# A 1x1 depthwise-separable layer on one core: chunk steps, weight loads in halves, a dummy matmul loop, ScalarE emptying PSUM, and a few stores in uneven pieces

## The chip, the cores and the metric

The kernel runs on one NeuronCore of a Trainium2 chip. The metric is the device time of one execution in microseconds (us). A run gives one such time; the number for the kernel is the median of several runs. Separately, one execution is recorded by the hardware profiler, and its span runs from the first to the last instruction of that execution.

## The reference

The input x has shape (1, 384, 384, 384) in bf16, dw is (1, 1, 384) and pw is (384, 384). Cut to what matters for a 1x1 depthwise kernel, the reference is:

```python
def reference(x, dw, pw):              # k = 1, pad = 0
    out = x * dw[0, 0][None, None, None, :]
    return jnp.einsum('bhwc,cd->bhwd', out, pw)
```

Each of the 147,456 pixels is a row of 384 channels; every channel is scaled by its dw, and the row is multiplied by the 384 x 384 matrix pw. The kernel folds dw into the rows of pw once, so that one matrix product of x with the scaled weights is left. x and the output are 113 MB each.

## The kernel before, in words

The pixels are cut into 288 supertiles of 512. Supertiles are grouped into chunks, which are the unit of DMA. `_chunks` gives the chunk sizes in supertiles: 1, 1, 2, 4, then 34 chunks of `LMAX` = 8, then 4, 2, 1, 1, which are 42 chunks. A chunk of x lies in one of three buffers `Xs`, a chunk of the output in one of three buffers `Os`. A full chunk is 3 MB in each direction.

SyncE (SP) issues the loads and stores of chunks. After the first three loads its order is written out: `load_x(t + 3)`, then `store(t)`, for t from 0. `load_x` (L95) waits on `s_t`, the semaphore of the last transpose of chunk t, since that frees the x buffer. `store` waits on `s_d` (L105) and `s_a` (L107), which say that VectorE and ScalarE have emptied PSUM for the chunk's last supertile. The completion of a store counts on `s_o`, and the engines wait for it before they write that output buffer again, three chunks later (L210, L211).

In a supertile the channels must come to the partitions. VectorE does this with 32 x 32 stream transposes of pairs of bf16 values read as uint32 (L174): two instructions for each supertile, h = 0 and h = 1, each for half of the six channel blocks, into one of two buffers `Ts`. TensorE then runs 48 matmuls per supertile (L134): six blocks, two parities of channel, four row groups q, each matmul with 32 rows and 384 columns. The four row groups work in the array beside each other and write four banks of PSUM. Even supertiles use one half of PSUM (`PS[0]`), odd ones the other. After the matmuls VectorE copies bank 3 to the output buffer (L212) and ScalarE copies banks 0 to 2 (L215), both casting to bf16.

TensorE's instructions are a hardware loop over pairs of supertiles. Ahead of a supertile's blocks 0 and 3 it waits for the transposes (`s_t`, L133); its first matmul waits on `s_a`, and the first matmul of row group 3 on `s_d`, so that PSUM is free. Every half of a supertile adds one to `s_pe`, for which the copies and the transposes wait.

Ahead of the loop the weights are made. Four DMAs of 288 KB (L89, two on SP, two on ScalarE's queue) bring pw to four groups of 32 partitions, a small one (L112) brings dw. VectorE spreads dw into `dwsel` (L186), transposes supertile 0, waits for all four weight DMAs, and makes six of the twelve scaled pieces `w_r` (L197); ScalarE makes the other six (L199). VectorE then transposes supertile 1. TensorE waits for all twelve pieces.

Of the kernel before, what the change touches and what calls it, by code (L numbers as in the profile page):

```python
# [7 lines left out]
BF16 = mybir.dt.bfloat16  # L8
F32 = mybir.dt.float32
U32 = mybir.dt.uint32  # L10
COPY = mybir.ActivationFunctionType.Copy

LMAX = 8
NX = 3
NO = 3


def _chunks(n_super: int):

    head, tail = [1, 1, 2, 4], [4, 2, 1, 1]  # L20
    mid = n_super - sum(head) - sum(tail)
    assert mid > 0 and mid % LMAX == 0
    return head + [LMAX] * (mid // LMAX) + tail
# [3 lines left out]
def kernel(  # L27
# [11 lines left out]
    nc = tc.nc  # L39
    P = nc.NUM_PARTITIONS  # L40
    B, H, W, C = x.shape
    assert dw.shape[0] == 1 and dw.shape[1] == 1, "only k=1 depthwise supported"
    D = pw.shape[1]
    N = B * H * W
    assert C == 384 and D == 384 and N % 1024 == 0
    NB = C // 64

    xf = x.rearrange("b h w c -> (b h w) c")
    of = out.rearrange("b h w d -> (b h w) d")

    NS = N // 512
    chunks = _chunks(NS)
    NT = len(chunks)
    s0 = [sum(chunks[:t]) for t in range(NT)]

    consts = ctx.enter_context(tc.tile_pool(name="consts", bufs=1))
# [3 lines left out]
    pw_r = consts.tile([P, NB, 2, D], BF16, name="pw_r")  # L60
    w_r = consts.tile([P, NB, 2, D], BF16, name="w_r")
    dwt = consts.tile([32, NB, 2], BF16, name="dwt")
    dwsel = consts.tile([P, NB * 2], F32, name="dwsel")
    warm = consts.tile([P, 3], F32, name="warm")
    seed = consts.tile([P, 2], F32, name="seed")

    Xs = [bufp.tile([P, 4 * LMAX, C], BF16, name=f"X{i}") for i in range(NX)]
    Ts = [bufp.tile([P, NB, 256], BF16, name=f"T{i}") for i in range(2)]
    Os = [bufp.tile([P, 4 * LMAX * D], BF16, name=f"O{i}") for i in range(NO)]
# [3 lines left out]
    s_t = [[nc.alloc_semaphore(f"s_t{i}{h}") for h in range(2)] for i in range(2)]  # L73
    s_pe = nc.alloc_semaphore("s_pe")
    s_a = [nc.alloc_semaphore(f"s_a{i}") for i in range(2)]
    s_d = [nc.alloc_semaphore(f"s_d{i}") for i in range(2)]
    s_o = [nc.alloc_semaphore(f"s_o{i}") for i in range(NO)]
    s_dw = nc.alloc_semaphore("s_dw")
    s_pw = nc.alloc_semaphore("s_pw")
    s_ds = nc.alloc_semaphore("s_ds")  # L80
    s_wr = nc.alloc_semaphore("s_wr")
    s_seed = nc.alloc_semaphore("s_seed")

    with tc.tile_critical():  # L84
        pw_v = pw.rearrange("(b w r) d -> w b (r d)", w=32, r=2)
        dw_v = dw.rearrange("a e (b w r) -> w (a e b) r", w=32, r=2)

        def load_pw(eng, q):
            eng.dma_start(pw_r[32 * q : 32 * q + 32].rearrange("w b r d -> w b (r d)"), pw_v).then_inc(s_pw, 16)  # L89

        def load_x(t):
            L = chunks[t]
            r = 512 * s0[t]
            src = xf[r : r + 512 * L, :].rearrange("(p s) c -> p (s c)", p=P)
            d = nc.sync.dma_start(Xs[t % NX][:, : 4 * L, :].rearrange("p s c -> p (s c)"), src)  # L95
            if t >= NX:
                je = s0[t - NX] + chunks[t - NX] - 1
                d._wait_ge(s_t[je % 2][1], je // 2 + 1)
            d.then_inc(s_x[t % NX], 16)

        def store(t):
            L = chunks[t]
            r = 512 * s0[t]
            je = s0[t] + L - 1
            nc.sync.wait_ge(s_d[je % 2], je // 2 + 2)  # L105
            dst = of[r : r + 512 * L, :].rearrange("(q p j) d -> p q (j d)", q=4, p=P)
            d = nc.sync.dma_start(dst, Os[t % NO][:, : 4 * L * D].rearrange("p (q e) -> p q e", q=4))  # L107
            d._wait_ge(s_a[je % 2], je // 2 + 2)
            d.then_inc(s_o[t % NO], 16)


        nc.scalar.dma_start(dwt[:], dw_v).then_inc(s_dw, 16)  # L112
        load_x(0)
        load_pw(nc.scalar, 2)
        load_pw(nc.sync, 0)
        load_pw(nc.scalar, 3)
        load_pw(nc.sync, 1)
        for t in range(1, NX):
            load_x(t)
        for t in range(NT):  # L120
            if t + NX < NT:
                load_x(t + NX)
            store(t)
        for o in range(NO):
            nc.sync.wait_ge(s_o[o], 16 * len(range(o, NT, NO)))


        def supertile(s, rv):
            for b in range(NB):
                for par in range(2):  # L130
                    for q in range(4):
                        if par == 0 and q == 0 and b in (0, 3):
                            nc.tensor.wait_ge(s_t[s][b // 3], rv)  # L133
                        mm = nc.tensor.matmul(  # L134
                            PS[s][:, q, :D],
                            lhsT=Ts[s][32 * q : 32 * q + 32, b, par::2],
                            rhs=w_r[32 * q : 32 * q + 32, b, par, :],
                            start=(b == 0 and par == 0),
                            stop=(b == NB - 1 and par == 1),
                            tile_position=(32 * q, 0),  # L140
                        )
                        if b == 0 and par == 0 and q == 0:
                            mm._wait_ge(s_a[s], rv)
                        elif b == 0 and par == 0 and q == 3:
                            mm._wait_ge(s_d[s], rv)
                        if b in (2, 5) and par == 1 and q == 3:
                            mm.then_inc(s_pe)

        nc.tensor.wait_ge(s_wr, 2 * NB)
        with nc.tensor.Fori(0, NS // 2, 1) as it:  # L150
            rv = nc.tensor.to_reg(it + 1)
            for s in range(2):
                supertile(s, rv)


        for s in range(2):
            nc.vector.memset(seed[:, s : s + 1], 0.0).then_inc(s_d[s])  # L157
        nc.gpsimd.memset(warm[:], 0.0).then_inc(s_seed)  # L158
        for s in range(2):
            c = nc.scalar.copy(warm[:, s + 1 : s + 2], warm[:, 0:1])  # L160
            if s == 0:
                c._wait_ge(s_seed, 1)
            c.then_inc(s_a[s])

        def transposes(t, j):
            jj = s0[t] + j
            L = chunks[t]
            s = jj % 2
            Xw = Xs[t % NX][:].bitcast(U32)[:, : 4 * L, :].rearrange("p (k l) c -> p k l c", l=L)
            Tw = Ts[s][:].bitcast(U32).rearrange("p b (i k) -> p b k i", k=4)  # L170
            for h in range(2):
                if h == 0 and j == 0:
                    nc.vector.wait_ge(s_x[t % NX], 16 * (t // NX + 1))  # L173
                ins = nc.vector.transpose(  # L174
                    out=Tw[:, 3 * h : 3 * h + 3],
                    in_=Xw[:, :, j, 96 * h : 96 * h + 96].rearrange("p k (b w) -> p b k w", w=32),
                )
                if jj >= 2:
                    ins._wait_ge(s_pe, 2 * (jj - 2) + h + 1)
                ins.then_inc(s_t[s][h])  # L180

        order = [(t, j) for t in range(NT) for j in range(chunks[t])]

        nc.vector.wait_ge(s_dw, 16)
        for q in range(4):
            nc.vector.tensor_copy(  # L186
                dwsel[32 * q : 32 * q + 32, :], dwt[:].rearrange("w b r -> w (b r)")
            ).then_inc(s_ds)
        transposes(*order[0])
        for b in range(NB):  # L190
            for r in range(2):
                eng = nc.vector if r == 0 else nc.scalar
                if b == 0:
                    eng.wait_ge(s_pw, 64)  # L194
                sc = dwsel[:, 2 * b + r : 2 * b + r + 1]
                if r == 0:
                    i = nc.vector.tensor_scalar_mul(w_r[:, b, r, :], pw_r[:, b, r, :], sc)  # L197
                else:
                    i = nc.scalar.activation(w_r[:, b, r, :], pw_r[:, b, r, :], COPY, scale=sc)  # L199
                if b == 0:  # L200
                    i._wait_ge(s_ds, 4)
                i.then_inc(s_wr)
        transposes(*order[1])

        for jj, (t, j) in enumerate(order):
            L = chunks[t]
            s = jj % 2
            Ov = Os[t % NO][:, : 4 * L * D].rearrange("p (q j d) -> p q j d", q=4, d=D)
            if j == 0 and t >= NO:
                nc.vector.wait_ge(s_o[t % NO], 16 * (t // NO))  # L210
                nc.scalar.wait_ge(s_o[t % NO], 16 * (t // NO))  # L211
            e = nc.vector.tensor_copy(Ov[:, 3, j, :], PS[s][:, 3, :D])  # L212
            e._wait_ge(s_pe, 2 * jj + 2)
            e.then_inc(s_d[s])
            a = nc.scalar.copy(Ov[:, 0:3, j, :], PS[s][:, 0:3, :D])  # L215
            a._wait_ge(s_pe, 2 * jj + 2)
            a.then_inc(s_a[s])
            if jj + 2 < NS:
                transposes(*order[jj + 2])


# [28 lines left out]
```

## Time and profile before

| | |
|---|---|
| median of 3 runs | 586.94 us (586.64 to 588.1) |
| profiled execution, own time | 585.78 us |
| profiled execution, span | 584.0 us |
| mean granted TensorE clock | 0.996 |
| moved by DMA | 227.79 MB, mean 390 GB/s |
| transposes on VectorE (L174) | 576, 449.1 us busy |
| casts on VectorE (L212) | 288, mean 558 ns |
| casts on ScalarE (L215) | 288, mean 1119 ns |
| store of a full chunk, issue to landing | median 23.0 us |
| load of a full chunk, issue to landing | median 17.9 us |

The page gives an engine's busy time as the union of its instructions' spans. In lines of the timeline the first number is the start in us from the span's start, the second the length; in brackets is how long the engine had been idle and who ended that. The chain of waits is followed back from the last instruction. "L134" is a line of the kernel as printed above. A DMA's time to landing runs from its issue until the last of its data is reported.

### The profile page before, as it was taken

To read this page: it belongs to the slowest core of one execution; us is meant where nothing else is said; L and a number is where in the kernel's file an instruction comes from. 1 tells how busy PE (TensorE), PEld (TensorE's weight loads), DVE (VectorE), ACT (ScalarE), POOL (GpSimd) and SP (SyncE) were. 2 spreads that over 40 slices of the span, in tenths; PEclk is the share of its full clock that TensorE was granted. 3 is DMA by queue.
4 is the path that set the end of the run, shared out by engine and by line. 5 is a ranking of instruction groups with operands and counts; after the bars stand their busy time and mean duration, and the time that the engine had idled before them with its cause. 6 is when DMAs were issued, how large, how long until landed. Compare 5 with 4: busy or idle time off the path is not lost.

```text
span 584.0 us, 29852 instructions
## 1 busy us (share of the span) xinstructions
PE 563.9 (97%) x13824; PEld 412.6 (71%) x13824; DVE 563.9 (97%) x876; ACT 326.9 (56%) x297; POOL 0.3 (0%) x5
## 2 busy tenths in 40 slices
PE   1999999999999999999999999999999999999995
PEld 0667777777777777777777777777777777777773
DVE  3899999999999999999999999999999999999995
ACT  3555555555555656565655555555555555555553
POOL 0000000000000000000000000000000000000000
PEclk9999999999999999999999999999999999999998
DMA  8799999999999999999999999999999999999858
GB/s 289 253 424 425 428 422 421 410 396 404 402 396 411 378 412 411 394 402 413 391 407 395 414 414 396 404 419 396 404 397 403 389 424 397 389 403 407 333 221 311
DMA packets 29277, 227.79 MB, mean 390 GB/s; under 512 B 1616, under 2 KB 5456, under 8 KB 24656
## 3 DMA queue, kind: packets, MB, share of 16 engines
q1 hardware_dynamic: 28640, 227.09, 97.1%
q10 hardware_dynamic: 624, 0.59, 0.4%
q14 instruction: 12, 0.10, 0.0%
q8 instruction: 1, 0.02, 0.0%
HBM read 114.43 MB, written 113.25 MB: 390 GB/s over the span
## 4 chain that ended last, share of the span: by engine, by line
PE 93%; DMA 5%; ACT 1%; SPq 0%; issue 0%; DVE 0%; ACTq 0%; DVEq 0%
PE ps L134 93%; DMA X<-in_x_dram 2%; DMA out_dram<-O 1%; DMA pw_r<-in_pw_dram 1%; ACT O L215 1%; ACT w_r L199 1%; DVE T L174 0%; SPq L89 0%; SPq L107 0%; SPq L95 0%; SPq L245 0%; DVEq L173 0%; ACTq L211 0%; ACTq L194 0%; SPq L84 0%
## 5 line engine op out<-in xcount | busy, mean ns | idle before, releaser
L134 PE MATMUL ps<-w_r,T 32*128 32x384 bf16 x13824 | 563.9, 322 | 13.8 <-ACT w_r L199 12.8
L134 PEld LDWEIGHTS ps<-w_r,T 32*128 32x128 bf16 x13824 | 412.6, 93 | 164.8 <-issue 14.4
L215 ACT CAST O<-ps 128x1152 bf16<-128x1152 f32 x288 | 322.2, 1119 | 245.2 <-PE ps L134 243.3
L174 DVE STREAM_TRANSPOSE T<-X 128x384 uint32<-128x384 uint32 x576 | 449.1, 856 | 1.6 <-DMA X<-in_x_dram 1.6
L212 DVE CAST O<-ps 128x384 bf16<-128x384 f32 x288 | 160.7, 558 | 6.8 <-PE ps L134 4.6
L199 ACT ACTIVATE w_r<-pw_r,dwsel 128x384 bf16<-128x384 bf16 x6 | 3.1, 601 | 5.4 <-DMA pw_r<-in_pw_dram 5.4
L186 DVE CAST dwsel<-dwt 32x12 f32<-32x12 bf16 x4 | 0.7, 163 | 3.9 <-DMA dwt<-in_dw_dram 3.8
L197 DVE TENSOR_SCALAR w_r<-pw_r,dwsel 128x384 bf16<-128x384 bf16 x6 | 1.5, 312 | 2.1 <-DMA pw_r<-in_pw_dram 2.1
L160 ACT ACT_TABLE_LOAD x1 | 1.3, 1283 | 2.3 <-issue 2.3
L157 DVE MEMSET seed<- 128x1 f32 x2 | 0.1, 59 | 1.0 <-SPq L84 1.0
L160 ACT COPY warm<-warm 128x1 f32<-128x1 f32 x2 | 0.3, 190 | 0.0
L234 POOL MEMSET const-bfloat16-1.0<- 128x1 bf16 x1 | 0.1, 102 | 0.0
L234 POOL MEMSET const-uint8-127<- 128x1 uint8 x1 | 0.1, 101 | 0.0
L158 POOL MEMSET warm<- 128x3 f32 x1 | 0.1, 100 | 0.5 <-SPq L84 0.5
L234 POOL MEMSET const-float32-0.0<- 128x1 f32 x1 | 0.1, 98 | 0.2 <-issue 0.2
L234 POOL MEMSET const-float32-1.0<- 128x1 f32 x1 | 0.1, 98 | 0.0
## 6 DMA issues: line engine op xcount, KB each, us to landing
X<-in_x_dram SPq DMA_DIRECT2D x34, 3072.0 KB, 17.9
out_dram<-O SPq DMA_DIRECT2D x34, 3072.0 KB, 23.0
X<-in_x_dram SPq DMA_DIRECT2D x2, 1536.0 KB, 12.4
out_dram<-O SPq DMA_DIRECT2D x2, 1536.0 KB, 13.5
X<-in_x_dram SPq DMA_DIRECT2D x4, 384.0 KB, 5.7
X<-in_x_dram SPq DMA_DIRECT2D x2, 768.0 KB, 10.1
out_dram<-O SPq DMA_DIRECT2D x4, 384.0 KB, 3.8
out_dram<-O SPq DMA_DIRECT2D x2, 768.0 KB, 11.3
```

Source lines behind the costliest of these rows:

```text
L134: mm = nc.tensor.matmul(PS[s][:, q, :D], lhsT=Ts[s][32 * q : 32 * q + 32, b, par::2], rhs=w_r[32 * q : 32 * q + 32, b, par, :], start=(b = ...
L157: nc.vector.memset(seed[:, s : s + 1], 0.0).then_inc(s_d[s])
L158: nc.gpsimd.memset(warm[:], 0.0).then_inc(s_seed)
L160: c = nc.scalar.copy(warm[:, s + 1 : s + 2], warm[:, 0:1])
L174: ins = nc.vector.transpose(out=Tw[:, 3 * h : 3 * h + 3], in_=Xw[:, :, j, 96 * h : 96 * h + 96].rearrange("p k (b w) -> p b k w", w=32),)
L186: nc.vector.tensor_copy(dwsel[32 * q : 32 * q + 32, :], dwt[:].rearrange("w b r -> w (b r)")).then_inc(s_ds)
L197: i = nc.vector.tensor_scalar_mul(w_r[:, b, r, :], pw_r[:, b, r, :], sc)
L199: i = nc.scalar.activation(w_r[:, b, r, :], pw_r[:, b, r, :], COPY, scale=sc)
L212: e = nc.vector.tensor_copy(Ov[:, 3, j, :], PS[s][:, 3, :D])
L215: a = nc.scalar.copy(Ov[:, 0:3, j, :], PS[s][:, 0:3, :D])
L234: nc = _bacc.Bacc("TRN2", target_bir_lowering=False, num_devices=1)
```

## The change

Six things are changed together.

- The chunk sizes become 1, 1, 2, 2, 3, 3, 4, then 32 chunks of 8, then 6, 4, 3, 2, 1, which are 44 chunks.
- pw is loaded in eight DMAs rather than four: each of the four partition groups gets blocks 0 to 2 and blocks 3 to 5 apart, with a semaphore for each half. VectorE makes nine of the twelve scaled pieces, ScalarE three; dwsel is spread by ScalarE. TensorE waits for a piece where it first uses it: in even supertiles the first row group's matmul of every block and parity carries such a wait.
- Ahead of its loop TensorE runs 11 times 8 matmuls on a tile of zeros, which GpSimd has set.
- ScalarE empties all four banks of a supertile. VectorE empties two banks of the very last supertile alone.
- The last chunk's store is cut in two, one part issued by SP, one by ScalarE.
- Of the chunks with eight supertiles those with t % 4 == 1 (eight chunks) are stored by four DMAs, of 112, 7, 7 and 2 partitions.

```diff
-    head, tail = [1, 1, 2, 4], [4, 2, 1, 1]
+    head, tail = [1, 1, 2, 2, 3, 3, 4], [6, 4, 3, 2, 1]
...
-        def load_pw(eng, q):
-            eng.dma_start(pw_r[32 * q : 32 * q + 32].rearrange("w b r d -> w b (r d)"), pw_v).then_inc(s_pw, 16)
+        def load_pw(eng, q, h):
+            bs = slice(3 * h, 3 * h + 3)
+            eng.dma_start(
+                pw_r[32 * q : 32 * q + 32, bs].rearrange("w b r d -> w b (r d)"), pw_v[:, bs]
+            ).then_inc(s_pw[h], 16)
...
+        parts = {t: [(0, P)] for t in range(NT)}
+        for t in range(NT):
+            if chunks[t] == LMAX and t % 4 == 1:
+                parts[t] = [(0, 112), (112, 119), (119, 126), (126, 128)]
...
-            nc.sync.wait_ge(s_d[je % 2], je // 2 + 2)
...
+            nc.sync.wait_ge(s_a[je % 2], je // 2 + 2)
+            for lo, hi in parts[t]:
+                nc.sync.dma_start(dst[lo:hi], src[lo:hi]).then_inc(s_o[t % NO], 16)
...
-        load_pw(nc.scalar, 2)
-        load_pw(nc.sync, 0)
-        load_pw(nc.scalar, 3)
-        load_pw(nc.sync, 1)
+        for h in range(2):
+            for q in range(2):
+                load_pw(nc.scalar, 2 + q, h)
+                load_pw(nc.sync, q, h)
...
+        nc.sync.dma_start(of_last[:, 2:4], o_last[:, 2:4])._wait_ge(s_d, 1).then_inc(
+            s_last, 16
+        )
...
+        wr_eng = {(b, r): int(r == 1 and b % 2 == 0) for b in range(NB) for r in range(2)}
...
                         if b == 0 and par == 0 and q == 0:
                             mm._wait_ge(s_a[s], rv)
-                        elif b == 0 and par == 0 and q == 3:
-                            mm._wait_ge(s_d[s], rv)
+                        elif s == 0 and q == 0:
+                            mm._wait_ge(*wr_done[b, par])
...
-        nc.tensor.wait_ge(s_wr, 2 * NB)
+        nc.tensor.wait_ge(s_zero, 1)
+        with nc.tensor.Fori(0, 11, 1) as _:
+            for i in range(8):
+                nc.tensor.matmul(
+                    PS[1][:, i % 4, :D],
+                    lhsT=zero[32 * (i % 4) : 32 * (i % 4) + 32, 0:P],
+                    rhs=zero[32 * (i % 4) : 32 * (i % 4) + 32, :],
+                    start=True,
+                    stop=True,
+                    tile_position=(32 * (i % 4), 0),
+                )
+        nc.tensor.wait_ge(*wr_done[0, 0])
...
+        nc.gpsimd.memset(zero[:].bitcast(U32), 0).then_inc(s_zero)
...
+        nc.scalar.wait_ge(s_dw, 16)
         for q in range(4):
-            nc.vector.tensor_copy(
-                dwsel[32 * q : 32 * q + 32, :], dwt[:].rearrange("w b r -> w (b r)")
-            ).then_inc(s_ds)
+            nc.scalar.copy(dwsel[32 * q : 32 * q + 32, :], dwt[:].rearrange("w b r -> w (b r)")).then_inc(s_ds)
...
-                nc.vector.wait_ge(s_o[t % NO], 16 * (t // NO))
-                nc.scalar.wait_ge(s_o[t % NO], 16 * (t // NO))
-            e = nc.vector.tensor_copy(Ov[:, 3, j, :], PS[s][:, 3, :D])
-            e._wait_ge(s_pe, 2 * jj + 2)
-            e.then_inc(s_d[s])
-            a = nc.scalar.copy(Ov[:, 0:3, j, :], PS[s][:, 0:3, :D])
+                nc.scalar.wait_ge(s_o[t % NO], o_count[t % NO][t // NO])
+            nq = 4
+            if jj + 1 == NS:
+                nq = 2
+                nc.vector.wait_ge(s_o[t % NO], o_count[t % NO][t // NO])
+                e = nc.vector.tensor_copy(Ov[:, nq:4, j, :], PS[s][:, nq:4, :D])
+                e._wait_ge(s_pe, 2 * jj + 2)
+                e.then_inc(s_d)
+            a = nc.scalar.copy(Ov[:, 0:nq, j, :], PS[s][:, 0:nq, :D])
...
+        nc.scalar.dma_start(of_last[:, 0:2], o_last[:, 0:2])._wait_ge(s_a[(NS - 1) % 2], (NS - 1) // 2 + 2).then_inc(
+            s_last, 16
+        )
```

## The prediction

> **What bounds the kernel now.** I read the page's busy times first.
>
> ```profile
> PE 563.9 (97%) x13824; PEld 412.6 (71%) x13824; DVE 563.9 (97%) x876; ACT 326.9 (56%) x297; POOL 0.3 (0%) x5
> ```
>
> TensorE and VectorE tie, and the DMA row is full as well, so this line alone doesn't say who leads. The timeline of a steady stretch does:
>
> ```profile
> 300.77 1.12 ACT L215 CAST O<-ps 128x1152 bf16<-128x1152 f32 x1 [0.83 <-PE ps L134]
> 300.77 0.56 DVE L212 CAST O<-ps 128x384 bf16<-128x384 f32 x1
> 301.24 1.56 DVE L174 STREAM_TRANSPOSE T<-X 128x384 uint32<-128x384 uint32 x2
> 302.72 1.12 ACT L215 CAST O<-ps 128x1152 bf16<-128x1152 f32 x1 [0.83 <-PE ps L134]
> 302.72 0.56 DVE L212 CAST O<-ps 128x384 bf16<-128x384 f32 x1
> ```
>
> VectorE's cast starts with ScalarE's, and ScalarE waited 0.83 us for TensorE: both are released by the same matmul, so TensorE paces. The pitch is 1.95 us a supertile. VectorE can go faster: just after the stall at 31 us its casts come at 31.83 and 33.67, a pitch of 1.84, so it has about 0.1 us to spare. Next the chain of waits in order of time, which shows where TensorE doesn't run:
>
> ```profile
> 1.88 7.37 DMA pw_r<-in_pw_dram
> ...
> 9.34 3.15 ACT w_r L199 x6
> 12.49 0.32 issue
> 12.81 4.02 PE ps L134 x42
> ...
> 18.45 11.88 DMA X<-in_x_dram
> ...
> 30.43 0.87 DVE T L174
> 31.30 0.14 issue
> 31.44 538.40 PE ps L134 x13248
> ...
> 571.01 7.67 DMA out_dram<-O
> ...
> 578.76 1.12 ACT O L215
> ```
>
> The reader is to see a head (weights land at 9.25, ScalarE scales six pieces until 12.49, the first supertile takes 4.02 instead of 1.95), one stall for x at 31.4, then 538 us of unbroken TensorE, and a tail where the last cast waits for an output buffer. 288 x 1.95 = 561.6 us can't be touched here; some 22 us around it can.
>
> Last, the stores' time from issue to landing, from the view of tile O for 40 to 100 us and for 400 to 520 us:
>
> ```profile
> DMA to landing us min/median/max: 18.9/19.5/19.7
> DMA to landing us min/median/max: 24.7/25.1/25.4
> ```
>
> Latency grows steadily although demand is constant. The trace's semaphore arrivals say why: of a store's 16 arrivals the last comes 0.5 us after the middle one for the store issued at 32 us, 1.3 at 48 us, 9.5 at 501 us. One DMA engine falls behind. Its arrivals for the 30 stores between 67.3 and 541.8 us are 15.82 us apart, while a full chunk is computed in 15.6. It hurts nothing yet: a load has two chunks (31.2 us) before it is needed, an output buffer as long.
>
> **What the Trainium skill says.** "TensorE: Matmul & The Clock Gate", Part 1, gives N/2.4 + 2.5 ns for a warm matmul and N/1.2 for a cold one: 162.5 ns for N = 384. Four row groups run together, so 12 x 162.5 = 1.95 us, exactly the trace's pitch; the cold first supertile (4.02) agrees with 12 x 320 = 3.84. "ScalarE: Activation LUTs", What ACT_TABLE_LOAD costs, gives 0.833 ns an element and 186 ns fixed: 1.146 us for 1152, trace 1.119. "DMA: Bandwidth & Descriptors", Why a DMA increments its semaphore by 16 and not by 1, says that a DMA from SP uses the largest k up to 16 engines that divides its outer dimension, the lowest-numbered ones; no DMA of 7 partitions is in this trace. The same page, Latency and other measured facts, says engines 7 and 15 are usually slower than the rest; it blames another kind of queue, and the trace gives no engine numbers, but one straggler of 16 fits.
>
> **The change, part by part.**
>
> *ScalarE empties PSUM.* VectorE loses 287 casts of 0.558 us. That work lay beside TensorE: worth nothing in the steady state. ScalarE's cast grows from 1152 to 1536 elements: 1.119 + 384 x 0.833 ns = 1.44 us (upper bound, in proportion, 1.49). TensorE wants the bank group back 1.95 us after ScalarE was released, so 0.45 us stays; cost 0. ScalarE is then at 74%. The wait for the cast of VectorE goes from TensorE and from SP. Transposes may now run earlier; TensorE was never late for them outside the one stall.
>
> *Waits on TensorE.* Eleven more on weights in every even supertile, 1584 in all, satisfied after the first pass. The four waits of a supertile today leave no mark, since 12 x 162.5 is all of the 1.95; less than 1 ns each, so 0 to 1.6 us. I take 0; cover is TensorE's own queue. No gain is possible.
>
> *Head.* Eight weight DMAs of half size instead of four; SP and ScalarE issue two more each, 0.45 us apiece, so loads of chunks 1 and 2 are issued 0.9 us later. The DMA engines are busy with weights until 9.25 anyway: 0. The dwsel copies go to ScalarE, which idles then (dwt lands at 4.9, ready near 5.9): 0. Chunk 0 lands at 5.2 and all weights at 9.25, so the first halves land about halfway, 7.2. VectorE makes nine scaled pieces at a pitch of 0.23 (six took 1.46 before), ScalarE three at 0.52. The dummy loop's 88 matmuls take at most 88 x 84 ns = 7.4 us cold (4.02/48 = 84 ns), less once warm; starting near 1.5 they end between 7 and 9. The first supertile starts near 8 and can't end before the last piece: second halves at 9.25, five VectorE pieces 9.35 to 10.5, supertile over at 10.9. A late dummy loop hides under that. The transpose for supertile 1 follows the pieces: 10.5 + 0.86, plus 0.14 to TensorE = **11.5**, where the second supertile starts. Before it started at 12.81 + 4.02 = 16.83. Gain 5.3, warm-up included.
>
> *Chunk steps.* 1,1,2,2,3,3,4 grow more slowly. The stall of 1.0 us at 31.4 came from an eight-supertile load issued at 18.45 and needed at supertile 8. Now chunk 4 (1.15 MB) is issued near 13, after store 0, and with it takes some 2.4 + 1.5 MB/0.41 = 6.1 us: 19.1, needed at 20.2. The first full chunk is issued near 25 and takes 11.9 as before: 37, needed at 39.5. Gain 1.0. In the tail 6,4,3,2,1 the last load gets five supertiles instead of three: the 0.3 us that TensorE waits at 575.6 goes. The last output buffer was issued for storing 7.8 us before it was wanted again and landed in 7.67; now there are six supertiles, 11.7 us. The last cast waited 1.92, of which 0.83 is usual: gain 1.1.
>
> *Last store.* Both engines take two banks: VectorE 0.558 + 384/0.96 ns = 0.96 instead of 1.12; half a store from each of two queues lands perhaps 0.15 us sooner. Gain 0.3.
>
> *Transfers of 7 partitions.* Eight chunks (9, 13, ... 37) store 112 partitions on 16 engines, twice 7 on the lowest seven, 2 on the lowest two. Engines 7 to 15 move 7/8 of their share, 0 to 6 nine or ten eighths. Three more issues of 0.39 us on SP delay the next load's wait, which ends 10 us later: 0. If the straggler is among the nine, it saves 7.9/8 = 1.0 us in four chunks, 15.82 becomes 15.57, and its backlog stays flat. The others managed a chunk in 14.75 while queues were full (middle arrivals 66 to 110 us); plus 0.25, or 0.5 for two, is below 15.6. Time gained in itself: 0, bounded by 2 us, since with the shorter head the straggler would otherwise be near the limit of the tail. What it could cost is rival B.
>
> Sum: 5.3 + 1.0 + 0.3 + 1.1 + 0.3 = 8.0. Span 584.0 - 8.0 = 576.0; own time of the profiled execution 585.78 - 8.0 = 577.8. The median of the runs (586.94) lies 1.2 above that execution, so I say **579.0**.
>
> **Rivals.** *A, a smaller head gain* (20%): if the half loads interleave and all land at 9.25, VectorE has nine pieces, +0.9; if loads run at the 253 GB/s of the early slices, chunk 4 lands near 21, +0.8 or more, and the first full chunk could add 1 to 2. Time 580 to 583. For it: x was late there before. Against: smaller chunks.
>
> *B, the straggler is one of the seven that get more* (7%). Then 15.82 becomes 16.07 a chunk, backlog grows 0.47 a chunk, store latency goes from 19 past the 31.2 us of the buffers after some 26 chunks, ScalarE waits for O, and the excess goes straight to the end: about 3 us in the stream, then three waits of about 2 us in the tail, where buffers turn over faster, and a final store behind a backlog: +10, so 589; with ten eighths 596. Point of decision: a store latency of 31 us. For it: the trace gives no number of the engine. Against: the skill's 7 and 15.
>
> *C, the 7-partition transfers run on all engines or help nobody* (8%): the straggler keeps 15.82, latency reaches about 25 as before; the tail of 16 supertiles at half the traffic drains it; 579 to 582.
>
> *Main case* 65%, 577.5 to 580.5.
>
> **How the numbers follow.** The range 577.0 to 583.5 takes in the main case, A, C and the unknown of the waits; B and 10% besides are left out. A measurement of this kernel can tell about 0.3% (1.8 us) from no change: faster means under 585.2. All but B are there: 0.89; B mostly slower, 0.07; between 0.04.
>
> **What would show it.** PE's first group of real matmuls at 8, second supertile at 11.5; CAST O<-ps on ScalarE 128x1536 near 1.44 us, pitch still 1.95; no wait of T for X in the head over 1 us; no wait of ScalarE for out_dram; store landing staying below 22 us late in the run. I'm wrong if the pitch exceeds 1.95, if landing passes 31 us, or if TensorE pauses between 11.5 and the end by more than 3 us.

## The result and the profile after

The changed kernel takes 624.52 us (median of four runs, 616.96 to 638.7), the kernel before 586.87. The ratio, in which here and below only executions within 1.5% of a kernel's fastest count, is 1.056, 95% interval 1.0496 to 1.0625: slower, by some 38 us between the medians, where 579.0 was forecast. The profiled execution of the changed kernel is the longest of the four (638.7 us); its times are therefore read for what happens and in which order, and the amounts are taken from the experiments.

The busy line of the page after the change:

```profile
PE 587.9 (92%) x13912; PEld 386.1 (61%) x13912; DVE 505.5 (79%) x586; ACT 416.5 (65%) x298; POOL 0.5 (0%) x6
```

Nobody is at 97% any more. The view of waits says for whom the time went (engine and line, for whom it waited, us in total, times, longest):

```profile
ACT O L256 <- DMA out_dram<-O: 54.3, 18, 5.0
PEld ps L162 <- ACT O L256: 46.0, 18, 4.5
```

ScalarE waits 54 us for output buffers that a store has not yet released, and TensorE waits behind ScalarE for PSUM. Before, ScalarE waited for a store once, at the end, for 1.9 us. The chain of waits has it in order of time (start, length, what):

```profile
11.99 201.06 PE ps L162 x4944
213.05 0.02 issue
213.07 1.45 ACT O L256
...
216.54 33.21 DMA out_dram<-O
249.79 0.04 issue
249.83 1.45 ACT O L256
251.28 0.05 issue
251.32 13.59 PE ps L162 x288
264.91 0.02 issue
264.93 1.45 ACT O L256
266.40 34.94 DMA out_dram<-O
```

The head went as forecast: the second supertile starts at 12 us, and TensorE then runs without a break for 201 us. After that the kernel lives from store to store: a store takes 33 to 42 us to land, which is more than the 31.2 us that an output buffer has, then TensorE runs some supertiles (a piece of 288 matmuls is six), and the next store is awaited. This pause costs more than its own length: six supertiles at 1.95 us are 11.7 us, but those from 251.32 us on take 13.59. The granted clock of TensorE, 1.00 from 12 to 213 us, is 0.89 from 250 to 265. SP, too, stands still while it issues the cut stores, here for 11 us (timeline of SP):

```profile
282.00 11.29 SPq L124 DMA_DIRECT2D out_dram<-O  x4
293.33 2.38 SPq L100 DMA_DIRECT2D X<-in_x_dram  x1
```

Loads of x share the engines with the stores and are the cleaner gauge. Their time from issue to landing, for 40 to 100 us and for 400 to 520 us, after the change:

```profile
DMA to landing us min/median/max: 17.8/17.8/17.9
DMA to landing us min/median/max: 28.4/33.8/35.3
```

The DMA engines, not TensorE, set the pace from 213 us on. One of them does. A full load has 16 semaphore arrivals, read here as one from each DMA engine when its share has landed. For the loads issued between 400 and 520 us the middle arrival comes 10 to 13 us after the issue, the last but one at 12 to 15, and only the last one at 28 to 35. That engine is called the late engine below.

### The profile page after: what moved, and what is told of

The parts are those of the page before. It is cut to its first block, busy times and chain, and to the rows that moved or that the text cites. A ratio compares the mean times of both kernels' runs of the same rounds, so it can differ in the third digit from the quotient of the medians.

```text
span 636.9 us, 29865 instructions
## 1 busy us (share of the span) xinstructions
PE 587.9 (92%) x13912; PEld 386.1 (61%) x13912; DVE 505.5 (79%) x586; ACT 416.5 (65%) x298; POOL 0.5 (0%) x6
## 4 chain that ended last, share of the span: by engine, by line
PE 49%; DMA 42%; SPq 4%; ACT 3%; DVE 1%; issue 0%; ACTq 0%; DVEq 0%
PE ps L162 49%; DMA out_dram<-O 37%; SPq L124 4%; DMA X<-in_x_dram 3%; ACT O L256 3%; DMA pw_r<-in_pw_dram 1%; DVE T L213 0%; SPq L92 0%; DVE w_r L234 0%; DVE O L253 0%; SPq L100 0%; ACTq L248 0%; SPq L289 0%; DVEq L212 0%; SPq L86 0%
## 5 line engine op out<-in xcount | busy, mean ns | idle before, releaser
L162 PE MATMUL ps<-w_r,T 32*128 32x384 bf16 x13824 | 581.8, 327 | 41.3 <-ACT O L256 36.7
L213 DVE STREAM_TRANSPOSE T<-X 128x384 uint32<-128x384 uint32 x576 | 502.4, 877 | 121.1 <-PE ps L162 55.7
L256 ACT CAST O<-ps 128x1536 bf16<-128x1536 f32 x288 | 412.4, 1437 | 208.6 <-PE ps L162 154.2
L162 PEld LDWEIGHTS ps<-w_r,T 32*128 32x128 bf16 x13824 | 382.9, 94 | 239.9 <-ACT O L256 46.0
L181 PE MATMUL ps<-zero 32*128 32x384 bf16 x88 | 6.1, 455 | 1.4 <-POOL zero L197 1.4
L181 PEld LDWEIGHTS ps<-zero 32*128 32x128 bf16 x88 | 3.2, 125 | 3.8 <-issue 1.6
L236 ACT ACTIVATE w_r<-pw_r,dwsel 128x384 bf16<-128x384 bf16 x3 | 1.7, 609 | 2.6 <-DMA pw_r<-in_pw_dram 2.6
## 6 DMA issues: line engine op xcount, KB each, us to landing
X<-in_x_dram SPq DMA_DIRECT2D x2, 1536.0 KB, 18.3
```

Source lines behind the costliest of these rows:

```text
L162: mm = nc.tensor.matmul(PS[s][:, q, :D], lhsT=Ts[s][32 * q : 32 * q + 32, b, par::2], rhs=w_r[32 * q : 32 * q + 32, b, par, :], start=(b = ...
L181: nc.tensor.matmul(PS[1][:, i % 4, :D], lhsT=zero[32 * (i % 4) : 32 * (i % 4) + 32, 0:P], rhs=zero[32 * (i % 4) : 32 * (i % 4) + 32, :], s ...
L213: ins = nc.vector.transpose(out=Tw[:, 3 * h : 3 * h + 3], in_=Xw[:, :, j, 96 * h : 96 * h + 96].rearrange("p k (b w) -> p b k w", w=32),)
L256: a = nc.scalar.copy(Ov[:, 0:nq, j, :], PS[s][:, 0:nq, :D])
```

## The experiments

The arrivals let one read the late engine's pace without any engine number: the time from the last arrival of one transfer to the last arrival of the next is what the late engine spent on it, as long as it always has work queued and stays the last. This is called its service time below. With whole stores it is 7.24 us for a full load and 8.40 for a full store at almost every chunk; 15.64 in all against the 15.6 in which a chunk is computed. Another engine takes about 7.40 us for a full store: that is the service time in stretches of the runs with 64 and 64 partitions and with fours below, where another engine is the last.

**Whole stores.** All of the change but the cut stores.

```diff
-                parts[t] = [(0, 112), (112, 119), (119, 126), (126, 128)]
+                parts[t] = [(0, P)]
```

> The changed kernel with every chunk stored whole (the 7-partition transfers undone, all else kept). If those transfers alone cost the time, this gives what the rest of the change was predicted to give: 577 to 583 us, TensorE's second supertile near 12 us, the store landing rising slowly as before. If ScalarE's emptying of PSUM or the waits on TensorE are to blame, it stays above 600 us.

578.4 us, ratio to before 0.9853 (0.983 to 0.9877). The cut stores alone cost the 46 us between this median and the changed kernel's, and the rest of the change brings what it was forecast to bring. Its chain of waits:

```profile
9.18 1.24 DVE w_r L234 x5
10.42 0.78 DVE T L213
11.20 0.14 issue
11.33 559.86 PE ps L162 x13776
571.18 0.02 issue
571.21 0.96 DVE O L253
```

One piece of 559.86 us for 287 supertiles is 1.9507 each: no stall between the second supertile and the last. The landing of its loads, for the same two stretches:

```profile
DMA to landing us min/median/max: 17.4/17.5/17.6
DMA to landing us min/median/max: 17.4/18.5/19.1
```

**Equal shares, two shapes.** The same eight chunks cut so that every engine still gets eight eighths.

```diff
-                parts[t] = [(0, 112), (112, 119), (119, 126), (126, 128)]
+                parts[t] = [(0, 112), (112, 128)]
```

> The same eight chunks stored as 112 and 16 partitions, both of which divide over 16 engines, so that no engine gets more than another. Share theory (the slow engine is one of the seven that carry nine eighths): as whole stores, 577 to 583 us. Shape theory (a transfer of 112 partitions, seven to an engine, runs slower in itself, since the engines then read partitions that cross each other's): most of the loss stays, 595 to 620 us, and the store of 112 takes the slow engine as long as 128 did or longer.

604.64 us, ratio 1.0298 (1.0226 to 1.0369). With `[(0, 64), (64, 128)]` instead:

> The same eight chunks stored as two transfers of 64 partitions, four to an engine. Share theory: as whole stores. Shape theory: as whole stores too, since four partitions to an engine don't cross; 577 to 583 us. A theory that any further transfer or issue on the queue costs time: above 585 us.

579.48 us, ratio 0.9871 (0.9846 to 0.9895), 1.1 us above whole stores. And with `[(0, 96), (96, 128)]`:

> The eight chunks stored as 96 and 32 partitions, six and two to an engine; every engine again carries eight eighths. If what 112 and 16 cost comes from an engine's partitions crossing groups of four (64 and 64 doesn't cross), this costs much the same, 595 to 615 us. If it needs the odd seven or the 16 neighbours on 16 engines, 577 to 583 us.

582.09 us (579.88 to 584.95), ratio 0.9911 (0.9883 to 0.9938), below the expected 595 to 615 of a theory of crossing partitions. So neither further transfers as such nor a share that isn't a multiple of four partitions cost the kernel much; 112 and 16 does.

The stores of 64 and 64 are not free for the engines, though. The first three take 10.1, 10.9 and 10.9 us, and after the first the middle arrival of the next load comes 19.0 us after its issue, where it is 13.4 with whole stores. But this delay falls on most engines alike. It shrinks by some 0.9 us a chunk until the next cut store, and the landing of stores never passes 26.4 us, so no output buffer is late.

The trace of 112 and 16 tells when the loss begins. The first four cut stores (89 to 277 us) hardly touch the late engine: service 9.12 and then 8.37 to 8.41, just the price of a whole store, with loads landing at 18.8 to 19.1. The fifth, issued at 339 us, takes 10.76; then the store issued at 385.7 us takes 13.39 and the landing of loads jumps from 22 to 28 us. That one is a whole store: it lies just ahead of a cut one, and the late engine works on it from 403 to 417 us, while the other engines, a store ahead, are at the cut store issued at 401.3. The landing of loads for 200 to 300, 300 to 400 and 400 to 520 us:

```profile
DMA to landing us min/median/max: 19.0/19.1/19.1
DMA to landing us min/median/max: 19.1/21.8/28.2
DMA to landing us min/median/max: 27.8/30.1/37.0
```

**Shares alone.** Whole stores; after those of the eight chunks, four loads of 7 partitions into a spare tile, which add work to the kernel that the reference doesn't need.

```diff
+            if L == LMAX and t % 4 == 1:
...
+                for i in range(4):
+                    lo = 7 * (4 * (g % 4) + i)
+                    more = xf[112 * i : 112 * i + 112, :].rearrange("(p s) c -> p (s c)", p=7)
+                    nc.sync.dma_start(extra[lo : lo + 7], more).then_inc(s_ex, 16)
```

> Whole stores, and behind each of the same eight chunks' stores four extra loads of 7 partitions (12 KB each) into a spare tile that nothing reads: the seven lowest engines get 49 KB or 1.8 us more in four chunks, and no store is uneven. Share theory (nine eighths on the slow engine is what hurts, whatever the shape): landing of stores climbs about 1.8 us in four chunks, from 21.5 past 31 us near the end, ScalarE waits for output buffers, 584 to 595 us. Shape theory (uneven stores must lie beside a lagging engine): landing climbs likewise, but a store never takes the slow engine longer than 8.4 us; 579 to 586 us.

612.97 us, ratio 1.0439 (1.042 to 1.0457): more than either theory allowed. No store is cut here, and a store's service stays at 8.3 to 8.7 to the end, as the shape theory had it. But the four loads issued ahead of 300 us that have extra loads with them take 9.07 to 10.02, where 7.24 and a quarter, 9.05, is the bytes' price, and once loads land later than about 25 us, those without extra work stretch as well, from 7.24 to 7.4 and up to 10. The landing of stores, for 40 to 100, 200 to 300 and 300 to 400 us:

```profile
DMA to landing us min/median/max: 18.7/19.2/20.4
DMA to landing us min/median/max: 24.5/26.6/31.2
DMA to landing us min/median/max: 31.3/34.7/37.0
```

The 31.2 us of an output buffer are passed at about 300 us, and ScalarE begins to wait. Extra work on seven engines, the late one among them, is enough by itself, without any cut store.

**Which engine.** One chunk alone is cut, into pieces that take part on ever fewer engines.

```diff
-            if chunks[t] == LMAX and t % 4 == 1:
-                parts[t] = [(0, 112), (112, 119), (119, 126), (126, 128)]
+            if t == 33:
+                parts[t] = [(0, 96), (96, 103), (103, 110), (110, 116), (116, 121), (121, 125), (125, 128)]
```

> One chunk alone (number 33) is stored as 96, 7, 7, 6, 5, 4 and 3 partitions. Transfers that include the slow engine land late, the others don't. If the lowest-numbered engines are used, the late arrivals count seven for engines 0 to 2, six for 3, five for 4, four for 5, three for 6 and one for 7 to 15. The change showed three late arrivals for 112, 7, 7 and 2, so 2 to 6. About 579 us.

579.47 us (one run). The late engine's load lands at 478.16 us; then its arrivals come at 484.43 (the 96 partitions: 6.27 us), 485.50, 486.55, 487.60 and 488.66, and its next load at 496.13. That is five: besides the 96 partitions it takes part in the pieces of 7, 7, 6 and 5, and not in those of 4 and 3. If a transfer takes the lowest-numbered engines first, the list above has five for number 4 and four for number 5, so this is number 4. In the changed kernel itself a cut store ends with three late arrivals (464.40, 465.59 and 466.52 for the one issued at 426.8 us): 112, 7 and 7, not the 2. The Trainium skill ("DMA: Bandwidth & Descriptors", Why a DMA increments its semaphore by 16 and not by 1) says that in a transfer issued by SP only the engines taking part add one each, that the issuing sequencer adds the rest at once, and that the engines are the lowest-numbered ones. The trace agrees on the counts: a cut store has 35 arrivals, 16 + 7 + 7 + 2 and three additions, which come within 2 us of the issue in the first (90.83, 91.23 and 91.54 for 89.74). It bears no engine number that could show the order.

**Who gets the rest.** 112 partitions as in the change, the other 16 as `[(112, 116), (116, 120), (120, 124), (124, 128)]`, so that engine 4 carries seven eighths.

> The changed kernel with the last 16 partitions of the same eight chunks as four transfers of 4 partitions, in place of 7, 7 and 2. By the run with seven sizes the slow engine takes part in transfers of 5 and more and not in those of 4 and less, so it now carries seven eighths. Share theory: the landing of loads falls in each such chunk and stays below 20 us, no wait for output buffers, 578 to 582 us. Shape theory (112 partitions is what hurts, whoever gets the rest): 600 to 620 us as with 112 and 16.

637.3 us, ratio 1.0833 (1.0777 to 1.0889). The forecast of the share theory, 578 to 582, is off by 55 us. In the trace the last engine's whole stores mostly take 7.38 to 7.42 us where no cut store is near, and the last arrivals of the cut store issued at 357.9 us come in steps of 0.93, an eighth of 7.40: it is no longer the slow engine that is last, but one of the four that got eleven eighths. The first cut store takes it at least 11.5 us, the second 18.3, where eleven eighths of 7.40 would be 10.2. With 5, 5, 5 and 1 partitions:

> The same with 5, 5, 5 and 1 partitions: one transfer fewer wide by one engine each, as many transfers as with fours. Now the slow engine takes part in all three and carries ten eighths. Share theory: worse than the change's nine eighths, above 625 us. If the number of further transfers is what costs, as with fours.

644.8 us, ratio 1.0991 (1.0906 to 1.1076). As many further transfers, and ten or eleven eighths for engines 0 to 4. Now the last engine's whole stores are back at 8.38 to 8.42 us away from the cut ones, and the cut store issued at 278.2 us ends with four late arrivals 1.05 us apart, 112, 5, 5 and 5. So the slow engine takes part in pieces of 5. It can't be among the four of the run with fours, since the engines that came last there need 7.40 us and not 8.40. That is number 4 again, on another chip than that of the run with seven sizes. Whichever engine is given more falls behind; relieving the slowest gains nothing while another is overloaded. Both runs keep the piece of 112, though, which with 16 beside it costs 26 us on its own, so what the share alone costs is not read from them.

**The kernel before with the cut stores.**

```diff
-            d = nc.sync.dma_start(dst, Os[t % NO][:, : 4 * L * D].rearrange("p (q e) -> p q e", q=4))
...
+            for lo, hi in parts[t]:
+                nc.sync.dma_start(dst[lo:hi], src[lo:hi]).then_inc(s_o[t % NO], 16)
```

> The kernel before with only the store of the full chunks with t % 4 == 1 cut into 112, 7, 7 and 2 partitions (nine chunks here), and the counts that this needs. If the transfers do the harm on their own, 605 to 630 us. If they need the shorter head or ScalarE alone at PSUM, within 1% of 587 us.

639.73 us, ratio 1.0907 (1.0871 to 1.0942), above the range expected. The harm needs nothing else of the change; nine chunks are cut here instead of eight.

**Fewer cut stores.** The change's own cut, in chunks 9 and 13 alone (`if t in (9, 13):`).

> The changed kernel with the 7-partition transfers in chunks 9 and 13 alone. In the changed kernel these two took the slow engine 2 us longer each and the other stores stayed at 8.4. If the collapse needs a lag that only builds up over more of them, loads land near 23 us from then on and nothing stalls: 578 to 581 us. If each such chunk costs its eighth of the loss, 590 us.

585.27 us, median of 20 runs from 578.84 to 589.83; ratio 0.9944 (0.9918 to 0.997). The two chunks cost nothing in some executions, 11 us in others, and anything between in the rest. In the profiled one (589.39) the two cut stores take 11.14 and 10.36 us; loads land at 23.6 after them, and although every later store is whole, the landing creeps on, a little more each chunk, to 30.2 at 476 us, because single loads take 7.3 to 8.5 us. Cuts of 112 and 16 in chunks 9, 13, 17 and 21 alone, and in 25, 29, 33 and 37 alone:

> Stores of 112 and 16 partitions in chunks 9, 13, 17 and 21 alone. With all eight the first four left no mark on the slow engine: its loads landed 19.1 us after issue before and after each. If an equal but split store only costs where the slow engine already lags by more than that, this equals the whole stores: 578 to 580 us. If every split store costs alike, half of the 26 us: about 591.

> The same in chunks 25, 29, 33 and 37 alone. With all eight the collapse began at chunk 25. If the first four prepared it by a lag that the trace hardly shows, this is near the whole stores, under 583 us. If late chunks alone are enough, since the slow engine's lag has grown by then anyway (18.5 us by 410 us with whole stores), 590 to 605.

The early four: median 578.7 us, ratio 0.9876 (0.9855 to 0.9897), but of 16 executions eleven lie at 578.2 to 579.9, one at 586.0 and four at 597 to 599. The late four: 578.56, 579.71, 589.34 and 603.15 us, too scattered to be compared. Neither of the alternatives that I had written down is what happened. An equal but cut store has no fixed price: in 11 of the 16 executions the early four cost nothing or next to nothing, in the others 8 to 21 us, and late ones can do the same. The profiled executions of both were short ones (578.32 and 578.56), so what happens in the long ones is not seen. With all eight every one of the four runs was over 600.

**Two terms of the gain.** Whole stores without the dummy loop (the wait on `s_zero` and the 88 matmuls left out):

> Whole stores and no dummy matmuls. The prediction counted the warm-up within the 5.3 us of the head. Cold, the first supertile takes 4 us from 7.6 and hides under the weights until 11; the clock rises after it or soon after: 0 to 2 us above the whole stores' 578.4, 578.4 to 580.5.

579.51 us, ratio 0.9872 (0.9856 to 0.9889): the warm-up is worth 1.1 us. Whole stores with the chunk sizes of before:

> Whole stores with the chunk sizes of before (1,1,2,4, eights, 4,2,1,1). The prediction priced the chunk steps at 1.0 + 0.3 + 1.1 = 2.4 us, which would be lost again: 580.8, range 579.5 to 584. With the earlier second supertile the load of the first full chunk is needed sooner, so the stall in the head may be more than the 1.0 of before.

580.9 us, ratio 0.991 (0.9892 to 0.9928): the chunk steps are worth 2.5 us. Its waits show that the tail's wait of ScalarE for an output buffer is back, and TensorE's wait for x in the head (through the transposes), which is 0.7 of the second line:

```profile
ACT O L256 <- DMA out_dram<-O: 1.3, 1, 1.3
PE ps L162 <- DVE T L213: 1.2, 2, 0.7
```

The best version is the one with whole stores, 578.4 us.

## Why the prediction was wrong, point by point

**Right: everything but the cut stores and one small term.** The gains summed to 8.0 us; the kernel with whole stores has a span of 576.5 against the 576.0 forecast and a median of 578.4 against 579.0. By terms: the second supertile starts at 11.33 (forecast 11.5); the first at 7.62 (near 8), with a first half of the weights at 6.9 (7.2); the dummy loop ends at 7.3; a cast of 1536 elements on ScalarE takes 1.439 us (1.44) and leaves the pitch at 1.95; the 1584 waits on weights leave no mark in the 559.86 us; no wait for output buffers in the tail; the chunk steps 2.5 us (2.4). The small term is the last store's 0.3 us. The last cast does take 0.96 us as forecast, but from its start to the landing of the last data it is 3.97 us, where it was 3.84 before: no gain. The weight halves and the waits on weights were not run apart from the rest. The timeline of a steady stretch, for comparison with the one shown before (ScalarE now idles 0.51 us where it idled 0.83):

```profile
300.16 1.44 ACT L256 CAST O<-ps 128x1536 bf16<-128x1536 f32 x1 [0.51 <-PE ps L162]
302.11 1.44 ACT L256 CAST O<-ps 128x1536 bf16<-128x1536 f32 x1 [0.51 <-PE ps L162]
```

**Wrong: the step "Transfers of 7 partitions ... Time gained in itself: 0, bounded by 2 us".** The step that was put at nothing cost 46 us. Two of its assumptions fell.

The first is the straggler's place. I took it to be among engines 7 to 15, since the Trainium skill ("DMA: Bandwidth & Descriptors", Latency and other measured facts) says that engines 7 and 15 are usually slower. The measurement decides otherwise: the straggler takes part in pieces of 7, 6 and 5 partitions and not of 4, which, with the lowest-numbered engines taken first, makes it number 4, among the seven that get more. That was rival B, given 7%. I had seen that the page blames another kind of queue and that the trace bore no number; a chance nearer to the count, seven engines of sixteen, was due, and not 7%.

The second is that a transfer costs its bytes. Rival B priced an uneven chunk at +1.0 us on the straggler, 0.47 a chunk with its drift, and the kernel at 589 to 596; it got the path and its point of decision right (store latency past 31.2 us, ScalarE waiting for O), and the size wrong. In the changed kernel's trace the late engine takes 10.6 to 10.9 us for the first three cut stores, +2.2 to +2.5 over 8.40, though nine eighths are only +1.05 (an eighth took it 1.05 in the run with seven sizes). Where its arrivals stand alone, the rest is mostly in the piece of 112: 8.59 us in the store issued at 214.5 us and 8.77 in the one at 426.8, where seven eighths of 8.40 are 7.35. The two pieces of 7 together take 2.27 and 2.12, near their bytes' 2.10.

From the load that lands at 103.15 us to the one at 529.21, 24 chunks later, the late engine needs 426.06 us, 71.0 for four chunks where 62.4 are computed: +8.6, against the +1.9 of rival B. The 426.06 us are 50.7 more than 24 chunks at 15.64. The six cut stores hold 15.3 of it, five whole stores that each lie just ahead of a cut one 18.0 (they take 10.95 to 13.2 us each), and the loads, stretched from 7.24 to as much as 9, hold 17.3. The price of the added bytes alone would be 6.3. Rival B's starting point of 15.82 a chunk was too high besides; with whole stores it is 15.64. The engine's slack, from a store latency of 21.8 us at 74 us to the 31.2 of the buffers, was 9.4 us; it was gone (32.1) at the store ahead of the third cut one.

A third point went unnoticed. I called the other engines safe, since they need 14.75 of 15.6 us a chunk. Four chunks leave 3.4 us; eleven eighths would add 2.8 by bytes, and yet those engines fell behind at once when they got them.

**What is shown and what isn't.** Shown: the cut stores are the whole loss; extra work on seven engines suffices without cut stores (613); equal shares in the shape 112 and 16 suffice with no engine given more than another (604.6). That shape alone costs 26 of the 46 us; how much the uneven share adds to it is not separated. Seen in the traces, but not taken apart by a run: the late engine's service time grows once it is far out of step with the rest, also on whole transfers. Three simple causes don't fit.

- Slow packets. In the traces' packet records most 6144-byte packets of stores take 234 ns. With whole stores 0.1% take more than 1.5 times that, after the change and with 112 and 16 it is 3%, with 64 and 64 it is 6%, with the extra loads 0.3%. The run with 6% lost 1.1 us, the one with 0.3% lost 35.
- SP's long issues. With 112 and 16 the cut stores issued at 338.86 and 401.26 us took SP 0.87 and 0.88 us, while the late engine already needed 10.76 us for the first of them and 13.39 for the store ahead of the second.
- TensorE's clock. In the changed kernel's trace the granted clock is 1.00 until the first waits.

Why a lagging engine gets slower is open. So is why 112 and 16 tips over where 96 and 32 hardly does, and why engine 4 is slower at stores.

## What to carry to other kernels

When sixteen DMA engines are within a few per cent of full, cut nothing unevenly: ask what the most loaded engine has to spare, and find by experiment which one is late before giving it more or less. Read the landing times by stretch of the run: a drift means a straggler, and its distance to the buffers' turnover time is all the slack there is, while past that point the loss can be several times what the added bytes cost (50.7 us against 6.3 above). A small cut can be free in one execution and cost 20 us in the next, so a few quick runs don't clear it.

## What the runs showed of the hardware that I had not expected

- One engine is slower at stores alone: 8.40 us against about 7.40 for its share of 3 MB, and level with the others at loads (7.24).
- An engine that lags far enough loses further time on whole transfers. The lag is the time from a load's middle arrival to its last. With whole stores it reaches 8 us, and loads stay at 7.24. In the run with two cut chunks, away from the cut stores, loads of 7.3 us and more appear from a lag of 12 us on. In the changed kernel, at 16 to 25 us, they take 7.2 to 9.0, and whole stores just ahead of a cut one 11 to 13 instead of 8.4.
- The issue of a narrow transfer held SP for up to 7.4 us (one of the four issues at 282 us above), where the same kernel's first ones took under 0.6. This was seen where an engine was far behind; the reason is not shown.
- The same program has short and long executions: 578 us and 597 to 599 with four early cuts. In the profiled long execution with two cut chunks (589.39) the lag goes on growing for some 300 us after the last cut.
